# A windowed attention and gated MLP kernel: loads in 1 KB runs, half-width chunks in pairs, another mask operation, layer-norm apply on GpSimd

## The chip, the cores and the metric

The kernel runs on one core of a Trainium2 chip. The time is the device time in microseconds of one execution; lower is better. The core has TensorE (PE), VectorE (DVE), ScalarE (ACT), GpSimd (POOL) and SyncE (SP), each with an instruction queue of its own that runs in the order of the program.

## The reference, cut to what matters

The inputs are float32; B=8 batches, H=8 heads, S=576 tokens, D=64. Attention looks back over 64 tokens only, and its output, heads side by side, goes through a spatial gating unit.

```python
scores = (q @ k^T) / sqrt(64)                # per batch and head, 576 x 576
mask   = (rel >= 0) & (rel < 64)             # rel = query position - key position
attn   = softmax(where(mask, scores, -1e9))
x      = attn @ v                            # heads side by side: (8, 576, 512)

h      = relu(x @ w_in)                      # (8, 576, 1024)
u, v   = h[..., :512], h[..., 512:]
v_n    = (v - mean(v)) / sqrt(var(v) + 1e-6) # over the 512 features
v_s    = w_spatial @ v_n + b_spatial         # mixes the 576 tokens
out    = (u * v_s) @ w_out                   # (8, 576, 512) float32
```

## The kernel before, in words

All of a batch's work is cut into units, and a list written out by hand gives each engine its order; nothing is scheduled at run time. The 576 tokens are four chunks of 128 and a remainder of 64; heads go in pairs, so that a batch has attention steps s=0 to 3 (two heads each, 512 tokens) and s=4 (the last 64 tokens of all heads).

Per batch b the units are:

- Loads: q, k and v come from DRAM in float32 on SP's queue (some of batch 0's v on ACT's). In DRAM a head's rows of 64 floats follow each other; a load puts token 128c+p on partition p, so each DMA moves runs of 256 bytes. Batches 0 and 1 are loaded head by head (`load_heads`, L68), later ones by chunk (`load_chunk`, L76). There are two buffers for each of q, k and v, in float32 (`NAT`) and in float16 (`F16`, names hq, hk, hv).
- Casts to float16 (`cast_pair` L81, `cast_chunk` L88), and a second copy hs of v that is moved by 64 tokens (`shift_pair` L93 and L94, `shift_half` L103 and L104), on POOL; batch 0 has its k casts on ACT and its q casts on DVE.
- T(b,s): PE transposes of k and q into the PSUM tile tp, which DVE copies to qk (L216).
- S(b,s): 16 small matmuls make the scores of key blocks of 64 tokens against at most 128 queries, in tile sc. E(b,s): ACT takes the exponential (L264), and DVE applies the mask by a `min` against a tile that holds 0 where a key isn't seen and 65504 where it is (L270).
- P(b,s): two matmuls with a matrix of ones (onesK, L281) sum the exponentials, and 16 matmuls of 64 columns (L290) multiply with v, both into oz. N1 and N2: ACT takes the logarithm of the sums and the exponential of minus that (L298, L306), and DVE multiplies (L308), which gives x.
- V(b,j), j=0 to 4: the half of the first product that is normalised, one chunk of tokens at a time; ACT's ReLU (L333) and DVE's `bn_stats` and `bn_aggr` (L335, L336). V(b,4) has only 64 tokens.
- LN(b): ACT takes Ln and Exp for the inverse deviations (L343, L344), then DVE applies the normalisation to the five chunks by a `tensor_scalar` each (L352, tiles vn).
- U(b,m): the other half (L362, L368) and its ReLU (L364). G(b,m): the product with the transposed w_spatial (wspT) and a row that adds the bias (L382, L390), then DVE multiplies with U's result. Each G reads all five vn.
- O(b,j): the last product (L403), a copy by ACT (L406) and the store (L407), which stands in ACT's queue for batches 0 and 1 and in SP's after that. O(b,4) has 64 tokens.

PSUM holds one tile each of tp, sc and oz, and three of tag mm, which V, U, G and O share. At the start PE also runs matmuls on a scratch tile (`warm`, L114).

Batch 0's attention comes first, then its V, W (the transposes of w_spatial), LN and U; then batch 1's attention with batch 0's G and O between the steps. In the main loop, iteration i has batch i's attention steps 0 to 4, and between them O of batch i-2 in step 0, V of batch a=i-1 in step 1, LN, U and the first G of batch i-1 in step 2, and the other U and G in steps 3 and 4. Loads and casts of batch i+1 are issued in the same iteration.

Of the kernel before, what the change touches and what calls it, by code (L numbers as in the profile page):

```python
# [13 lines left out]
B = 8  # L14
S = 576
BIG = 65504.0


@with_exitstack
def kernel(  # L20
# [31 lines left out]

    NAT = {}
    F16 = {}

# [8 lines left out]
    SRC = (q, k, v)  # L64

    def load_heads(b, x, h0, eng):
        for h in (h0, h0 + 1):
            eng.dma_start(NAT[b][x][:, 0:4, h, :],  # L68
                          SRC[x][b, h, 0:512, :].rearrange("(c p) d -> p c d", p=128))
# [4 lines left out]
    def load_chunk(b, x, c):  # L74
        sn = 128 if c < 4 else 64
        nc.sync.dma_start(NAT[b][x][0:sn, c, :, :],  # L76
                          SRC[x][b, :, 128 * c:128 * c + sn, :].transpose([1, 0, 2]))

    def cast_pair(b, x, p, eng):
        hs = slice(2 * p, 2 * p + 2)  # L80
        eng.tensor_copy(F16[b][x][:, 0:4, hs, :], NAT[b][x][:, 0:4, hs, :])  # L81

    def cast_rem(b, x, eng):
        eng.tensor_copy(F16[b][x][0:64, 4, :, :], NAT[b][x][0:64, 4, :, :])

    def cast_chunk(b, x, c, eng):
        sn = 128 if c < 4 else 64
        eng.tensor_copy(F16[b][x][0:sn, c, :, :], NAT[b][x][0:sn, c, :, :])  # L88
# [7 lines left out]
    def shift_rem(b, eng):  # L96
        eng.tensor_copy(F16[b][3][0:64, 4, :, :], F16[b][2][0:64, 4, :, :])

    def shift_half(b, half, eng):
        vn, vs = F16[b][2], F16[b][3]  # L100
        c = 2 * half
        if half < 2:
            eng.tensor_copy(vs[0:64, c:c + 2, :, :], vn[0:64, c:c + 2, :, :])  # L103
            eng.tensor_copy(vs[64:128, c + 1:c + 3, :, :], vn[64:128, c:c + 2, :, :])  # L104
        else:
            eng.tensor_copy(vs[0:64, 4, :, :], vn[0:64, 4, :, :])
# [9 lines left out]
    def load_by_pairs(b):  # L116
        new_batch(b)
        for p in range(4):
            for x in (1, 0, 2):
                load_heads(b, x, 2 * p, nc.scalar if (b == 0 and p < 2 and x == 2) else nc.sync)  # L120
        for x in (1, 0, 2):
            load_rem(b, x, nc.sync)

    load_by_pairs(0)
    new_half(0)
    warm(16)
# [16 lines left out]
    mask = cpool.tile([128, 2, 8, 64], f16, name="mask")  # L143
    maskr = cpool.tile([128, 8, 64], f16, name="maskr")
    for h in (0, 1):
        for u in range(8):
            if u % 2 == 1:
                nc.vector.tensor_copy(mask[:, h, u, :], keep[:])
            else:
                nc.vector.tensor_scalar(mask[:, h, u, :], keep[:], -1.0, BIG, ALU.mult, ALU.add)  # L150
        nc.vector.memset(mask[64:128, h, 0, :], 0.0)
    for u in range(8):
        nc.vector.tensor_copy(maskr[:, u, :], mask[:, 0, 2, :])
# [4 lines left out]
    for i in range(NSB):  # L158
        nc.vector.memset(mv_t[i][:], 1.0)
        nc.vector.memset(vn4_t[i][64:65, :], 1.0)  # L160

    def casts_step(b, s, engk, engq):
        if s < 4:
            cast_pair(b, 1, s, engk)
            cast_pair(b, 0, s, engq)
            cast_pair(b, 2, s, nc.gpsimd)
            shift_pair(b, s, nc.gpsimd)
        else:
            for x in (1, 0, 2):
                cast_rem(b, x, nc.gpsimd)  # L170
            shift_rem(b, nc.gpsimd)

    class _Act:
        @staticmethod
        def tensor_copy(o, i):
            nc.scalar.copy(o, i)  # L176
# [4 lines left out]
    wsp_nat = [cpool.tile([128, 576], f16, name=f"wnat{t}") for t in range(5)]  # L181
# [6 lines left out]
    def load_wsp():  # L188
        for t in range(5):
            tn = 128 if t < 4 else 64  # L190
            nc.gpsimd.dma_start(wsp_nat[t][0:tn, :], moe_w_spatial[128 * t:128 * t + tn, :])
        nc.gpsimd.dma_start(wspT[4][64:65, 0:576], moe_b_spatial[:].unsqueeze(0))
# [9 lines left out]
    X = {}  # L202

    def emit_T(b, s):
        tp = psp.tile([128, 1024], f16, tag="tp", bufs=1, name=f"tp{b}_{s}")
        Qh, Kh = F16[b][0], F16[b][1]
        with nc.named_scope(f"T{b}_{s}"):
            if s < 4:
# [7 lines left out]
                nc.vector.tensor_copy(qk[:, :], tp[:, :])  # L216
# [11 lines left out]
    SC = {}  # L228

    def emit_S(b, s):  # L230
# [3 lines left out]
        with nc.named_scope(f"S{b}_{s}"):  # L234
            if s < 4:
                for kap in range(8):
                    r = 64 * (kap % 2)
                    c0 = 0 if kap == 1 else 64 * kap
                    c1 = min(512, 64 * kap + 128)
                    for h in (0, 1):  # L240
                        d = slice(64 * h, 64 * h + 64)
                        nc.tensor.matmul(sc[r:r + 64, h, c0:c1],  # L242
                                         qk[d, 512 + 64 * kap:576 + 64 * kap], qk[d, c0:c1],
                                         start=True, stop=True)
            else:
                for p in range(4):
                    for h in (0, 1):
                        d = slice(64 * h, 64 * h + 64)
                        qs = qk[d, 64 * p:64 * p + 64]
                        nc.tensor.matmul(sc[0:64, h, 64 * p:64 * p + 64],  # L250
                                         qk[d, 256 + 64 * p:320 + 64 * p], qs,
                                         start=True, stop=True)
                    for h in (0, 1):
                        d = slice(64 * h, 64 * h + 64)
                        qs = qk[d, 64 * p:64 * p + 64]
                        nc.tensor.matmul(sc[64:128, h, 64 * p:64 * p + 64],
                                         QK[b, p][d, 960:1024], qs,
                                         start=True, stop=True)

    def emit_E(b, s):  # L260
        sc = SC.pop((b, s))
        if s < 4:
            e2 = apool.tile([128, 2, 512], f16, tag="e2", bufs=2, name=f"e2_{b}_{s}")
            nc.scalar.activation(e2[:, :, :], sc[:, :, :], AF.Exp, bias=0.0, scale=0.125)  # L264
            m = mask[:, :, :, :].rearrange("p h u w -> p h (u w)")
# [52 lines left out]
    G = {}  # L318
# [245 lines left out]
```

The softmax here doesn't subtract the row's maximum and nothing guards it: scores larger than these inputs give would overflow.

## Time and profile before

| | |
|---|---|
| three runs | 250.28, 251.56, 252.69 us; median 251.56 us |
| the profiled execution | 251.05 us, of which its instructions span 249.3 us |
| mean granted clock of PE | 0.962 of full speed |
| busy: PE, DVE, ACT, POOL | 227.3, 155.3, 152.2, 122.1 us |
| moved by DMA | 40.41 MB in 120014 packets, 113776 of them under 512 bytes |

Busy shares are means over stages that have different limits. A busy PE is one whose queue had a matmul in flight; the granted clock tells how fast it went. "x" ahead of a number is a count of instructions, an arrow with a name in square brackets tells what ended an idle time.

### The profile page before, as it was taken

To read this page: it belongs to the slowest core of one execution; us is meant where nothing else is said; L and a number is where in the kernel's file an instruction comes from. 1 tells how busy PE (TensorE), PEld (TensorE's weight loads), DVE (VectorE), ACT (ScalarE), POOL (GpSimd) and SP (SyncE) were. 2 spreads that over 40 slices of the span, in tenths; PEclk is the share of its full clock that TensorE was granted. 3 is DMA by queue.
4 is the path that set the end of the run, shared out by engine and by line. 5 is a ranking of instruction groups with operands and counts; after the bars stand their busy time and mean duration, and the time that the engine had idled before them with its cause. 6 is when DMAs were issued, how large, how long until landed. Compare 5 with 4: busy or idle time off the path is not lost.

```text
span 249.3 us, 6391 instructions
## 1 busy us (share of the span) xinstructions
PE 227.3 (91%) x2588; PEld 116.8 (47%) x2588; DVE 155.3 (62%) x317; ACT 152.2 (61%) x266; POOL 122.1 (49%) x183
## 2 busy tenths in 40 slices
PE   7784996996399999999999999999999999999893
PEld 3442453553254464436544554455445544553351
DVE  6453277562459782887479556966597659755630
ACT  3373484446447666766785577756776677767423
POOL 3469638875499695369016592469135900000000
PEclk9999799799569999999999999999999999999998
DMA  8999999999999996992389948995499040014005
GB/s 159 218 184 208 216 204 229 191 201 276 249 199 210 198 178 175 246 206 52 128 192 211 192 128 221 189 198 135 137 216 156 27 165 5 3 42 149 0 3 189
DMA packets 120014, 40.41 MB, mean 162 GB/s; under 512 B 113776, under 2 KB 114864, under 8 KB 119984
## 3 DMA queue, kind: packets, MB, share of 16 engines
q1 hardware_dynamic: 114720, 34.88, 70.1%
q0 software_dynamic: 1840, 2.24, 5.2%
q10 hardware_dynamic: 3424, 2.88, 4.1%
q8 instruction: 20, 0.33, 0.6%
q14 instruction: 10, 0.08, 0.1%
HBM read 32.79 MB, written 9.44 MB: 169 GB/s over the span
## 4 chain that ended last, share of the span: by engine, by line
PE 60%; DVE 13%; ACT 9%; DMA 8%; SPq 3%; POOL 2%; issue 2%; ACTq 1%; POOLq 0%
SPq L68 3%; DMA nv_80<-in_v_dram 2%; DMA out_dram<-ob_0_1033 2%; DMA out_dram<-ob_1_3433 2%; DMA nq_78<-in_q_dram 2%; ACTq L407 1%; PE ps_0_804 L382 1%; PE warm_583 L114 1%; PE pv_0_1308 L330 1%; PE ps_0_4590 L382 1%; PE ps_0_4237 L382 1%; DVE mv_172 L336 1%; PE ps_0_3720 L382 1%; PE ps_1_895 L382 0%; PE ps_3_4653 L382 0%
## 5 line engine op out<-in xcount | busy, mean ns | idle before, releaser
L88 POOL CAST hq_2281<-nq_2285 128x512 f16<-128x512 f32 (+1 forms) x5 | 3.2, 635 | 12.8 <-DMA nq_2285<-in_q_dram 12.8
L114 PEld LDWEIGHTS <-scratch 128*128 128x128 f16 x51 | 5.0, 112 | 7.3 <-issue 3.8
L88 POOL CAST hq_3389<-nq_3393 128x512 f16<-128x512 f32 (+1 forms) x5 | 3.9, 797 | 8.8 <-DMA nq_3393<-in_q_dram 8.8
L281 PEld LDWEIGHTS <-onesK 128*64 128x64 f16 x80 | 4.6, 107 | 7.5 <-issue 5.2
L88 POOL CAST hq_2835<-nq_2839 128x512 f16<-128x512 f32 (+1 forms) x5 | 3.6, 720 | 8.3 <-DMA nq_2839<-in_q_dram 8.3
L176 ACT CAST hk_109<-nk_79 128x512 f16<-128x512 f32 x4 | 2.5, 618 | 7.5 <-DMA nk_79<-in_k_dram 7.5
L114 PE MATMUL warm_113<-scratch 128*128 128x512 f16 x16 | 5.5, 524 | 1.3 <-DVE scratch L109 1.3
L81 POOL CAST hv_110<-nv_80 128x512 f16<-128x512 f32 x4 | 2.5, 632 | 8.3 <-DMA nv_80<-in_v_dram 7.3
L88 POOL CAST hv_1729<-nv_1733 128x512 f16<-128x512 f32 (+1 forms) x5 | 3.5, 708 | 4.4 <-DMA nv_1733<-in_v_dram 4.4
L88 POOL CAST hq_1727<-nq_1731 128x512 f16<-128x512 f32 (+1 forms) x5 | 2.9, 609 | 4.6 <-DMA nq_1731<-in_q_dram 4.6
L88 POOL CAST hv_2283<-nv_2287 128x512 f16<-128x512 f32 (+1 forms) x5 | 3.2, 637 | 3.8 <-DMA nv_2287<-in_v_dram 3.8
L81 POOL CAST hv_433<-nv_437 128x512 f16<-128x512 f32 x4 | 2.5, 613 | 5.2 <-DMA nv_437<-in_v_dram 5.1
L88 POOL CAST hv_1184<-nv_764 128x512 f16<-128x512 f32 (+1 forms) x5 | 3.1, 611 | 3.9 <-DMA nv_764<-in_v_dram 3.9
L362 PEld LDWEIGHTS <-win_181 128*128 128x128 f16 x32 | 3.1, 98 | 3.8
L362 PEld LDWEIGHTS <-win_182 128*128 128x128 f16 x32 | 3.1, 98 | 3.8
L88 POOL CAST hv_1220<-nv_1224 128x512 f16<-128x512 f32 (+1 forms) x5 | 3.9, 780 | 2.0 <-DMA nv_1224<-in_v_dram 2.0
L88 POOL CAST hq_1182<-nq_762 128x512 f16<-128x512 f32 (+1 forms) x5 | 3.3, 654 | 3.2 <-DMA nq_762<-in_q_dram 2.7
L81 DVE CAST hq_108<-nq_78 128x512 f16<-128x512 f32 x4 | 1.7, 432 | 4.8 <-DMA nq_78<-in_q_dram 4.8
L281 PE MATMUL oz_3_1153<-e_1_3_1108,onesK 128*64 128x512 f16 x2 | 0.6, 611 | 4.4 <-DVE x_2_1133 L308 4.4
L88 POOL CAST hv_3391<-nv_3395 128x512 f16<-128x512 f32 (+1 forms) x5 | 3.0, 611 | 2.8 <-DMA nv_3395<-in_v_dram 2.8
L88 POOL CAST hv_2837<-nv_2841 128x512 f16<-128x512 f32 (+1 forms) x5 | 3.3, 666 | 2.0 <-DMA nv_2841<-in_v_dram 1.8
L264 ACT ACTIVATE e_1_0_831<-sc_0_813 128x1024 f16<-128x1024 f32 x1 | 1.0, 1023 | 5.2 <-PE sc_0_813 L242 5.2
(1871 smaller groups left out, 940.3 us busy)
## 6 DMA issues: line engine op xcount, KB each, us to landing
nk_79<-in_k_dram SPq DMA_DIRECT2D x9, 128.0 KB, 3.9
nq_78<-in_q_dram SPq DMA_DIRECT2D x9, 128.0 KB, 4.1
nk_436<-in_k_dram SPq DMA_DIRECT2D x9, 128.0 KB, 4.8
nq_435<-in_q_dram SPq DMA_DIRECT2D x9, 128.0 KB, 4.8
nv_437<-in_v_dram SPq DMA_DIRECT2D x9, 128.0 KB, 4.1
nk_763<-in_k_dram SPq DMA_DIRECT2D x4, 256.0 KB, 5.5
nq_762<-in_q_dram SPq DMA_DIRECT2D x4, 256.0 KB, 5.7
nv_764<-in_v_dram SPq DMA_DIRECT2D x4, 256.0 KB, 6.0
```

Of the source, the lines that this page charges most:

```text
L68: eng.dma_start(NAT[b][x][:, 0:4, h, :], SRC[x][b, h, 0:512, :].rearrange("(c p) d -> p c d", p=128))
L81: eng.tensor_copy(F16[b][x][:, 0:4, hs, :], NAT[b][x][:, 0:4, hs, :])
L88: eng.tensor_copy(F16[b][x][0:sn, c, :, :], NAT[b][x][0:sn, c, :, :])
L114: nc.tensor.matmul(t[:, :], scratch[:, 0:128], scratch[:, :], start=True, stop=True)
L176: nc.scalar.copy(o, i)
L264: nc.scalar.activation(e2[:, :, :], sc[:, :, :], AF.Exp, bias=0.0, scale=0.125)
L281: nc.tensor.matmul(oz[64 * h:64 * h + 64, 1, 0:n], onesK[:, :], e2[:, h, 0:n], start=True, stop=True)
L330: nc.tensor.matmul(pv[0:jn, :], xcol(b, r, j), w_in_sb[r][:, 512:1024], start=(r == 0), stop=(r == 3))
L336: nc.vector.bn_aggr(mv_t[b % NSB][0:jn, j, :], st6[0:jn, 0:6])
L362: nc.tensor.matmul(pu[:, :], w_in_sb[r][:, 128 * m:128 * m + 128], X[b, r][:, :], start=(r == 0), stop=(r == 3))
L382: nc.tensor.matmul(ps[:, :], VN[b, kk][0:kn, 128 * m:128 * m + 128], wspT[kk][0:kn, 0:512], start=(kk == 0), stop=(kk == 4))
L407: (nc.scalar if b < 2 else nc.sync).dma_start(out[b, 128 * j:128 * j + jn, :], ob[0:jn, :])
```

## The change

It changes the layout of the loads, the order of the units, and the engine or operation of three steps:

- q of all batches, and k of batches 0 to 2 (`KRUNS = 3`), are loaded so that partition p holds tokens 4p to 4p+3 of a head, one run of 1 KB. Casts of such tensors go head by head. So tokens of q stand in another order (4p+j in column 128j+p); scores, masks, x, w_spatial and the output rows follow that order: S and P's matmuls with v read and write four runs instead of one, DVE copies k's transposes in two parts for those batches, the transposes of w_spatial read every fourth column, and the store writes rows 4p+j. w_spatial's first 512 rows come in one DMA, and the bias goes through a tile brow and two ACT copies.
- Loads go out one iteration earlier (batch i+2's in iteration i); casts go by head pairs in all batches, batch 2's during batch 1's attention.
- V(a,4) and O(o,4) become one unit VO4 with the two products on the two halves of one PSUM tile. O's other chunks and V are spread over steps 0 to 2, and all G are in steps 3 and 4.
- The mask is applied by `scalar_tensor_tensor` (max with 0, then min with the mask).
- LN is applied as v*rs+nb, with nb = -mean*rs from a small DVE instruction, and on POOL for all batches but 0.

```diff
+    def in_runs(b, x):
+        return x == 0 or (x == 1 and b < KRUNS)
+
+    def load_runs(b, x, h0, n, eng):
+        eng.dma_start(NAT[b][x][:, 0:4, :, :].rearrange("p j h d -> p (j h d)")
+                      .rearrange("p (h e) -> p h e", h=8)[:, h0:h0 + n, :],
+                      SRC[x][b, h0:h0 + n, 0:512, :].rearrange("h (p j) d -> p h (j d)", j=4))
...
     def cast_pair(b, x, p, eng):
-        hs = slice(2 * p, 2 * p + 2)
-        eng.tensor_copy(F16[b][x][:, 0:4, hs, :], NAT[b][x][:, 0:4, hs, :])
+        if in_runs(b, x):
+            src = NAT[b][x][:, 0:4, :, :].rearrange("p j h d -> p (j h d)") \
+                .rearrange("p (h j d) -> p j h d", h=8, j=4)
+            for h in (2 * p, 2 * p + 1):
+                copy_on(eng, F16[b][x][:, 0:4, h, :], src[:, :, h, :])
+        else:
+            hs = slice(2 * p, 2 * p + 2)
+            copy_on(eng, F16[b][x][:, 0:4, hs, :], NAT[b][x][:, 0:4, hs, :])
...
-                nc.vector.tensor_copy(qk[:, :], tp[:, :])
+                if in_runs(b, 1):
+                    nc.vector.tensor_copy(qk[:, 512:1024].rearrange("d (p j) -> d p j", j=4),
+                                          tp[:, 512:1024].rearrange("d (j p) -> d p j", j=4))
+                    nc.vector.tensor_copy(qk[:, 0:512], tp[:, 0:512])
+                else:
+                    nc.vector.tensor_copy(qk[:, :], tp[:, :])
...
-        nc.vector.tensor_tensor(e2[:, :, :], e2[:, :, :], m, ALU.min)
+        nc.vector.scalar_tensor_tensor(e2[:, :, :], e2[:, :, :], 0.0, m, ALU.max, ALU.min)
...
+    def emit_VO4(a, o):
+        pv = mm(f"pvo{a}_{o}")
+            for r in range(4):
+                if a is not None:
+                    nc.tensor.matmul(pv[0:64, :], X[a, 4][:, 64 * r:64 * r + 64],
+                                     w_in_sb[r][:, 512:1024], start=(r == 0), stop=(r == 3))
+                if o is not None:
+                    nc.tensor.matmul(pv[64:128, :], G[o, 4][:, 64 * r:64 * r + 64],
+                                     w_out_sb[r][:, :], start=(r == 0), stop=(r == 3))
+        if a is not None:
+            v_tail(a, 4, pv)             # ReLU, bn_stats, bn_aggr
+        if o is not None:
+            nc.scalar.copy(ob[64:128, :], pv[64:128, :])
+            store_eng(o).dma_start(out[o, 512:576, :], ob[64:128, :])
...
-            nc.vector.tensor_scalar(vn[0:jn, :], vs[0:jn, :], mv[0:jn, j, 0:1],
-                                    rs[0:jn, j:j + 1], ALU.subtract, ALU.mult)
+            (nc.vector if b < 1 else nc.gpsimd).tensor_scalar(
+                vn[0:jn, :], vs[0:jn, :], rs[0:jn, j:j + 1], nb[0:jn, j:j + 1], ALU.mult, ALU.add)
...
     # main loop, iteration i with a = i - 1, o = i - 2 (o > 0, a < B)
+            st[0] += Os(o, (0, 1)) + Vs_(a, (0, 1))
+            st[1] += Vs_(a, (2, 3)) + [lambda: emit_VO4(a, o)] + Os(o, (2,))
+            st[2] += [lambda: emit_LN(a)] + Os(o, (3,)) + Us(a, (0, 1, 2))
+            st[3] += Gs(a, (0,)) + Us(a, (3,)) + Gs(a, (1,)) + Us(a, (4,))
+            st[4] += Gs(a, (2, 3, 4))
+        loads = load_units(i + 2)        # four of them ahead of each step
+        casts = cast_units(i + 1)        # step s: head pair s; in step 2 they stand ahead of LN
```

The line numbers L81 to L407 above are those of the kernel before. In the changed kernel the mask is L300, the layer-norm apply L400, the small instruction for nb L392, the copies of qk L245, L247 and L249, the casts L119 and the shifts L137 and L138.

## The prediction, made before the changed kernel was run

> **What bounds the kernel now.** I read the page's busy shares and slices first, then the busy time by stretches, then PE's timeline in one steady iteration, then POOL's timeline and the DMA queues.
>
> ```profile
> span 249.3 us, 6391 instructions
> PE 227.3 (91%) x2588; PEld 116.8 (47%) x2588; DVE 155.3 (62%) x317; ACT 152.2 (61%) x266; POOL 122.1 (49%) x183
> ...
> PEclk9999799799569999999999999999999999999998
> DMA  8999999999999996992389948995499040014005
> ```
> ```profile
> 42.00:68.00 26.00, 20.11 (x272) 11.56 (x272) 11.98 (x20) 12.72 (x20) 16.83 (x27) 0.84 1.20 229
> 68.00:92.70 24.70, 24.02 (x303) 13.35 (x303) 18.65 (x35) 15.25 (x27) 21.33 (x27) 0.89 1.10 203
> ...
> 118.90:145.00 26.10, 25.65 (x315) 13.27 (x314) 18.42 (x36) 18.16 (x33) 9.44 (x14) 1.00 0.96 183
> ```
> The first columns are the stretch and its length, then busy time of PE, PEld, DVE, ACT, POOL, PE's granted clock, DMA share, GB/s. From 92.7 us on PE is busy 98% at full clock: iterations i=3 to 6 of the main loop take 26.0 us each (92.7 to 196.7), i=7 24.6, the tail 28.0. Before that the DMA engines are never idle, at about 200 GB/s, and PE waits and loses clock. So there are two stages with different limits: a stream of loads up to 92.7, and PE after it.
>
> ```profile
> 126.69 0.41 PE L281 MATMUL oz_0_2456<-e_4_0_2358,onesK 128*64 128x512 f16 x2
> 126.93 0.23 PE L290 MATMUL oz_0_2456<-e_4_0_2358,hv_1729 128*64 128x64 f16 x4
> ...
> 129.11 0.40 PE L330 MATMUL pv_4_2507<-win_179,x_4_2383 128*64 128x512 f16 x1
> 129.35 0.38 PE L330 MATMUL pv_4_2507<-win_180,x_4_2383 128*64 128x512 f16 x1
> ...
> 133.34 0.39 PE L382 MATMUL ps_0_2612<-wspT_192,vn_0_2544 128*128 128x512 f16 x1
> 133.67 0.39 PE L382 MATMUL ps_0_2612<-wspT_193,vn_1_2546 128*128 128x512 f16 x1
> 134.28 0.39 PE L382 MATMUL ps_0_2612<-wspT_194,vn_2_2548 128*128 128x512 f16 x1 [0.23 <-DVE vn_2_2548 L352]
> 134.60 0.39 PE L382 MATMUL ps_0_2612<-wspT_195,vn_3_2550 128*128 128x512 f16 x1
> 135.22 0.39 PE L382 MATMUL ps_0_2612<-wspT_196,vn_1_174 65*128 65x512 f16 x1 [0.23 <-DVE vn_1_174 L352]
> ```
> Full-width matmuls of 512 columns start 0.216 us apart. The two onesK matmuls, each 64 columns of the array and writing opposite halves of PSUM, together hold PE only from 126.69 to 126.93: 0.24 us for two. So half-width pairs run side by side, while V4 and O4 alone (one half each) still pay 0.216 a matmul. And G0 takes 2.2 us from 133.34 to 135.54 instead of 1.08: it waits for the five vn from DVE.
>
> **The change by parts.**
>
> *Pairing (VO4).* O4 or V4 costs four matmuls and a pause of 0.09 at the switch of width, 0.95 us. As a pair one of them vanishes, seven times (o=0 to 6); in i=3 to 7 and in the tail this is on PE's path: -0.95 each. Its ReLU, bn_stats, output copy and store remain, the store on ACT's queue for o<2 and else SP's.
>
> *Later need for vn.* G moves from step 2 to step 3, so that after VO4 PE has O2, T, O3, S and P, U0 to U2 and T4 first: 0.87+0.45+0.87+1.0+2.6+0.35, about 6.3 us with switches, before G0 starts.
>
> *Layer-norm apply on POOL (L400).* Five DVE tensor_scalars (start spacing 0.33, or 0.70 beside POOL) go away for batches 1 to 7, one small DVE nb is added (0.15, by the aggregate's 0.18). POOL's price for it is not in the trace. Nearest rows: a 128x512 POOL cast 0.61; affine_select 0.24 for 64 and 0.29 for 128 columns, a slope of 0.8 ns a column, 0.60 for 512. Lower end 0.61; upper end a second pass over the data, 0.18+2x0.43=1.03 (0.61 and the 1.03 of a 64x1024 copy give fixed 0.18 and 0.43 per 512). I take 0.65: it streams one tensor like the cast.
>
> The Trainium skill speaks against this (GPSIMD Engine Reference, § 3.1): software loops there reach 1.8 cycles an element at best above two operations, 0.77 us for 512 elements; by that estimate each of seven LNs would be 0.6 us later and the sum 4 us worse. The casts' 0.61 is faster than that loop, so the row decides.
>
> *Is vn in time?* With t0 at a step-0 T, PE reaches VO4's end at 8.9. ACT then has relu, the output copy, ln, O2's copy and zi before Ln and Exp: rs at 12.1. DVE has x and the qk copy ahead of nb: 13.0. POOL from 13.1 at 0.65: vn4 at 16.4, wanted by G0's fifth matmul at 16.1. But POOL's queue holds the casts of steps 0 to 2 in front. Per pair: k 0.61, q two casts of 256 elements (0.40 each by that slope), v 0.61, two shifts 1.22: 3.24 us; the shift of pair 0 waits for P(i-1,4) at about 3.0. 3.0+1.2+2x3.24=10.7, inside 13.0 if little is lost to DVE. So G0 stalls 0.2 at best, 1.1 more for each mask that holds POOL up. I take 0.7 against 1.1 now. Behind LN on POOL stand casts of steps 3 and 4 (5.7 us); T(i+1,3), four steps or some 19 us later, needs them, and that covers them; loads now go out a whole iteration ahead on SP's queue, so the stores queued between them cost nothing.
>
> *Mask op (L300).* The f16 tensor_tensor shows 0.69 (starts 0.60 apart). No row shows a scalar_tensor_tensor; ends 0.60 and 1.13 (the 0.60 that 512 f32 elements take, less fixed 0.07, doubled, plus 0.07), I take 1.13: +0.53 on DVE, four times an iteration, against 5x0.33 to 0.70 saved; DVE stays near 18 of 25 us. Exp's end to P's use leaves 3 us now, so +0.5 is hidden; without that cover it costs 0.5 a step.
>
> ```profile
> 87.19 1.32 DVE L270 TENSOR_TENSOR e_2_3_1589<-e_2_3_1589,mask 128x1024 f16<-128x1024 f16 x1 [0.73 <-ACT e_2_3_1589 L264]
> ...
> 88.03 1.39 POOL L104 COPY hs_1221<-hv_1220 64x1024 f16<-64x1024 f16 x1
> ```
> Here a mask beside a POOL copy takes 1.32 instead of 0.69, and the next copy 1.39 instead of 1.03: they exclude each other. The Trainium skill (SBUF — State Buffer, § Who interferes with whom) says that any DVE op with two SBUF inputs contends with a POOL op that reads SBUF; the new op still has two, so by the rule a mask would now hold POOL 1.1 us and the stall would be 1.3, by which the sum would be some 3 us worse.
>
> *Four-run streams.* S and PV matmuls read and write four runs of 16 or 32 instead of one. No row shows it; ends are today's 0.35+0.27 a step and twice that. I take today's: the column count is unchanged.
>
> *k's two copies (L245, L247)* for batches 0 to 2: 0.60+0.33 against 0.60 on DVE, idle half of that stage. Bias copies on ACT (about 0.8) ahead of LN(0), masks behind the first q cast (about 1 us), fewer and larger weight DMAs: all in the fill, hidden by the stream below; uncovered, 2 us.
>
> *1 KB runs.*
> ```profile
> q1 hardware_dynamic: 18774, 4.72, 107.5%
> q10 hardware_dynamic: 656, 1.18, 13.4%
> ```
> This is the DMA view of 44 to 70 us: 256-byte packets (q1) take 24 ns each, 2 KB stores (q10, 576 of them) 97 ns. On a line between them a 1 KB packet takes 55, so 1.74 times the bytes a second: 348 GB/s against 200. q or k of a batch (1.05 MB) then needs 3.0 us instead of 5.2. Ends: 200 (no gain) and 490 (q1's 4.72 MB at 200 fill 23.6 of the 26 us, which leaves 2.4 for the stores' 1.18 MB).
>
> **The fill, which now ends on POOL.** Batch 3's last v lands at 86 now:
> ```profile
> 86.38 0.61 POOL L88 CAST hv_1220<-nv_1224 64x512 f16<-64x512 f32 x1 [0.18 <-DMA nv_1224<-in_v_dram]
> ```
> Seven tensors (q of batches 0 to 3, k of 0 to 2) gain 2.2 us: 70.4, its last chunk 69.4. v is still loaded by chunks and cast by pairs, so pair 0's v cast waits for all of it, and LN(1) stands in POOL's queue behind pairs 0 to 2 of batch 3: 69.4+0.61+1.22+2x3.24=77.7, five vn 81.0, G0(1) done 81.3. PE would have been there at about 70 (T(2,1) at 58: POOL's last cast for batch 2 waits for v landing at about 52). After G0 come 8 us of PE work plus 1.9 for a clock lost in the 11 us pause (42.65 to 46.2 now shows such a stretch at 0.43 spacing): i=3 starts at 91.2, now 92.7: -1.5. So most of the faster load is handed back as POOL's wait. Ends: without gain in rate 107 (+14); at 490 POOL's own work allows LN(1) at 70, i=3 at 83 (-10).
>
> **Sum.** Fill -1.5; i=3 to 6: -(0.95+0.4)x4=-5.4; i=7 -1.0; tail -0.95 for the pair and nothing net for LN (DVE's 0.33 becomes 0.65, more PE work lies before G0). Total -8.8: span 249.3 to 240.5, the profiled run 251.05 (1.75 outside the span) to 242.2, and against the median of 251.56, 242.8.
>
> **Rivals.**
> *LN on POOL becomes the bound (slower).* Place: vn before G0. Each 0.1 us on L400 costs 0.5 in seven places (LN(1), i=3 to 7, tail), 3.5 us; it takes the gain away from 0.90 us an op; at 1.03 it is 13.3-8.8=+4.5, 256.1. For: POOL's queue is nearly full (15.4 casts, 3.3 LN, some 4 lost to masks, of 25). Against: one-input rows stream at 0.8 ns. 14%.
> *POOL keeps up in the fill*: i=3 at 83, 8 us more gained: 234.6. For: stores seem nearly free beside loads. Against: three batches of casts in line. 22%.
> *1 KB runs no faster* (the change doesn't do what it says): i=3 at 107, +15.6: 258.4. For: HBM or issue could be the limit; against: SP issues 256 KB in 1.05 us unblocked but needs 1.2 here, so the engines are slow. 8%.
> *Four-run streams at twice the time*: 0.62x4x5=+12.4: 255.2. 6%.
>
> **Numbers.** Forecast 50%, its own range 237 to 249. The range 231 to 257 adds the quick fill and most of the POOL case. A measurement here tells about 1%, so faster is under 249.0: forecast and quick fill and a small part of the POOL case, 0.76; within 1% 0.08; slower 0.16.
>
> **What would show it.** Right: L400 near 0.65; POOL idle before a v cast of batch 3 ended by DMA; G0(1) waiting several us for POOL; po_0_ of iteration 3 near 91; later iterations near 24.7 with G0 close to 1.8; both halves of VO4 in 0.9 us. Wrong: L400 above 0.9, S groups longer than 0.35, or batch 3 landing far from 70.

## The result and the profile after

The changed kernel is slower. Its four runs took 259.86 to 262.98 us, median 261.61, against 250.92 for the kernel before beside it: a ratio of 1.041, 95% interval 1.032 to 1.051. The prediction was 242.8, range 231 to 257. Here and below the times are medians of all runs, while ratios and their intervals leave out the executions in a second, slower state, some per cent longer. The profiled execution took 260.86 us, of which its instructions span 259.1.

The first and second parts of the page of the changed kernel:

```profile
span 259.1 us, 6474 instructions
PE 220.0 (85%) x2586; PEld 117.0 (45%) x2586; DVE 165.8 (64%) x298; ACT 152.3 (59%) x272; POOL 172.8 (67%) x275
...
DMA  7999999999999809990587858680220023002304
```

PE is busy for 7.3 us less than before (at 0.95 each, seven pairs make 6.7 of it), and the span is 9.8 us longer: PE waits more. The DMA engines' first empty slice is the fifteenth, 91 to 97 us, so that from there on loads don't hold the rest up. POOL went from 122 to 173 us of work. Two stretches of the same kernel show it by stage (columns: length, busy PE, PEld, DVE, ACT, POOL, PE's granted clock, DMA share, GB/s):

```profile
73.00:99.45 26.45, 23.44 (x300) 12.15 (x299) 19.21 (x33) 16.18 (x29) 24.01 (x38) 0.90 0.78 168
...
129.30:155.40 26.10, 24.19 (x315) 13.21 (x314) 18.82 (x32) 17.84 (x32) 22.06 (x33) 1.00 0.74 183
```

In the first stretch, which is i=2, POOL is busy for 24 of 26 us. The second is one steady iteration, from S(4,0) to S(5,0). It takes 26.1 us like before, with 24.2 of PE work instead of 25.7. So the pair's gain is there and is waited away.

The table gives the start of some S groups and the span, all from PE's timelines, for this kernel, the one before and the experiments; "steady" is a third of S(4,0) to S(7,0).

| | S(0,1) | S(1,0) | S(2,0) | S(3,0) | S(4,0) | S(7,0) | span | steady |
|---|---|---|---|---|---|---|---|---|
| before | 11.8 | 44.8 | 69.3 | 94.4 | 120.5 | 198.3 | 249.3 | 25.9 |
| changed | 14.8 | 49.7 | 75.9 | 101.3 | 129.3 | 207.7 | 259.1 | 26.1 |
| e1 | 14.8 | 47.0 | 70.0 | 95.0 | 123.5 | 200.2 | 249.0 | 25.6 |
| e2 | 13.7 | 44.8 | 71.2 | 99.5 | 127.3 | 203.5 | 254.1 | 25.4 |
| e3 | 12.9 | 44.1 | 75.5 | 100.9 | 129.3 | 207.7 | 259.1 | 26.1 |
| e4 | 14.3 | 46.9 | 70.6 | 94.7 | 122.5 | 197.0 | 245.5 | 24.8 |
| e5 | 14.1 | 45.3 | 70.5 | 100.8 | 129.1 | 210.1 | 261.0 | 27.0 |
| e6 | 14.3 | 47.0 | 71.9 | 93.8 | 118.2 | 189.4 | 236.9 | 23.7 |
| e7 | 13.6 | 45.2 | 72.0 | 94.1 | 117.8 | 189.0 | 236.9 | 23.7 |
| e10 | 14.8 | 47.5 | 70.5 | 94.6 | 120.2 | 196.8 | 245.3 | 25.5 |
| e11 | 14.3 | 46.6 | 69.6 | 92.1 | 115.8 | 187.0 | 234.5 | 23.7 |
| e12 | 11.2 | 43.7 | 70.3 | 92.4 | 116.1 | 187.3 | 234.8 | 23.7 |
| e13 | 11.6 | 44.2 | 65.6 | 86.9 | 110.9 | 182.1 | 229.2 | 23.7 |
| e14 | 11.9 | 43.3 | 67.6 | 89.1 | 113.6 | 184.8 | 231.8 | 23.7 |

Of the 9.8 us that the changed kernel is late at the end, 6.9 are there at S(3,0) and 1.9 more at S(4,0). Less than 1 us is added after that.

Each row is one execution, and its start varies. Up to S(2,0) the changed kernel, e1 and e5 have the same instructions in the same order. Yet S(1,0) comes at 49.7, 47.0 and 45.3 us in them and S(2,0) at 75.9, 70.0 and 70.5. Part of it is ACT's fourth copy of batch 0's output, which waits for the first store to land in the changed kernel and waits for nothing in e1:

```profile
68.14 0.59 ACT L455 COPY ob_3_1152<-po_3_1146 128x512 f32<-128x512 f32 x1 [3.34 <-DMA out_dram<-ob_0_1059]
```
```profile
62.65 0.58 ACT L455 COPY ob<-po 128x512 f32<-128x512 f32 x1
```

So a difference of a few us between two rows at S(1,0) or S(2,0) shows nothing by itself. The steady column and the medians over the runs are firmer. The places where time is lost are three.

**A steady iteration on PE** (i=4; the timeline's columns are start, duration, engine, line, operation; the bracket is the idle time ahead and what ended it):

```profile
134.97 0.38 PE L373 MATMUL pvo_2_2510<-win_139,x_4_2423 128*64 128x512 f16 x1
135.00 0.38 PE L376 MATMUL pvo_2_2510<-wout_143,g_4_2310 128*64 128x512 f16 x1
...
135.97 0.39 PE L452 MATMUL po_2_2530<-wout_143,g_0_2127 128*128 128x512 f16 x1
...
139.73 0.41 PE L311 MATMUL oz_1_2607<-e_4_1_2507,onesK 128*64 128x512 f16 x2 [1.07 <-DVE x_0_2541 L339]
...
143.35 0.39 PE L430 MATMUL ps_0_2680<-wspT_150,vn_0_2571 128*128 128x512 f16 x1
...
144.57 0.39 PE L430 MATMUL ps_0_2680<-wspT_153,vn_3_2577 128*128 128x512 f16 x1 [0.36 <-POOL vn_3_2577 L400]
145.31 0.39 PE L430 MATMUL ps_0_2680<-wspT_154,vn_1_138 65*128 65x512 f16 x1 [0.36 <-POOL vn_1_138 L400]
```

The halves of VO4 start 0.03 us apart, and O2 starts at 135.97: two units in 1.0 us. But P(4,1) then waits 1.07 us for x_0, because there is one oz tile and x_0 is the last reader of the P before. And G0 takes 2.2 us, from 143.35 to the start of the next unit at 145.54, where five matmuls need 1.08: 1.1 us of waiting for vn, just as before the change. So 0.95 is gained and 1.07 is lost, with 0.2 more for x_4 ahead of P(4,0).

**LN of the same iteration on POOL:**

```profile
140.52 0.77 POOL L400 TENSOR_SCALAR vn_0_2571<-vs_0_2403,rs_2566,nb_2567 128x512 f16<-128x512 f16 x1 [0.71 <-DVE nb_2567 L392]
141.27 1.73 POOL L400 TENSOR_SCALAR vn_1_2573<-vs_1_2416,rs_2566,nb_2567 128x512 f16<-128x512 f16 x1
...
144.50 0.76 POOL L400 TENSOR_SCALAR vn_1_138<-vs_4_2520,rs_2566,nb_2567 64x512 f16<-64x512 f16 x1
```
```profile
140.83 1.54 DVE L300 SCALAR_TENSOR_TENSOR e_4_2_2627<-e_4_2_2627,mask 128x1024 f16<-128x1024 f16 x1 [0.48 <-ACT e_4_2_2627 L294]
```

One apply takes 0.77 us, and in every LN but the last one of them is held up to 1.6 to 1.8 us, by the mask that DVE starts meanwhile (the second fence): the apply that starts at 141.27 ends 0.63 us after the mask does. All five take 4.7 us instead of the 3.3 of the prediction.

**Why x_0 is late** is seen on ACT, in the same iteration:

```profile
136.13 0.59 ACT L354 ACTIVATE vs_4_2520<-pvo_2_2510 64x512 f16<-64x512 f32 x1 [0.48 <-PE pvo_2_2510 L376]
136.75 0.58 ACT L382 COPY ob_4_2525<-pvo_2_2510 64x512 f32<-64x512 f32 x1
137.35 0.60 ACT L329 ACTIVATE ln_0_2528<-oz_0_2487 128x512 f32<-128x512 f32 x1
137.85 0.58 ACT L455 COPY ob_2_2536<-po_2_2530 128x512 f32<-128x512 f32 x1
138.31 0.64 ACT L337 ACTIVATE zi_0_2539<-ln_0_2528 128x512 f32<-128x512 f32 x1
```

P(4,0) is done at 135.0, but N1 (ln_0) stands in ACT's queue behind VO4's ReLU and output copy, and N2 (zi_0) behind O2's copy. In iterations 2 and 3 the stores are issued on ACT too, and the same wait is 2.1 to 2.2 us.

**The start** (POOL's timeline from the landing of batch 2's v to the first LN on POOL):

```profile
56.52 0.62 POOL L119 CAST hv_784<-nv_608 128x512 f16<-128x512 f32 x1 [7.65 <-DMA nv_608<-in_v_dram]
...
73.32 0.61 POOL L119 CAST hk_1232<-nk_794 128x512 f16<-128x512 f32 x1
...
75.05 0.62 POOL L119 CAST hv_1233<-nv_795 128x512 f16<-128x512 f32 x1 [0.43 <-PE pv_0_1260 L364]
...
78.12 1.48 POOL L119 CAST hk_1232<-nk_794 128x512 f16<-128x512 f32 x1
...
82.25 1.48 POOL L119 CAST hk_1232<-nk_794 128x512 f16<-128x512 f32 x1
...
86.52 1.58 POOL L400 TENSOR_SCALAR vn_0_1460<-vs_0_1266,rs_1455,nb_1456 128x512 f16<-128x512 f16 x1 [0.21 <-DVE nb_1456 L392]
```

From 56.5 POOL has only 1.8 us of idle time until LN(1). (The profile puts the 0.43 us ahead of the cast at 75.05 down to PE. But the last chunk of batch 3's v, which this cast needs, was issued at 69.5, and at the 5.3 us that such a load takes it landed at about 74.8, so that this wait may have been for the load.) Three pairs of batch 3 take 13.0 us, 73.3 to 86.3, or 4.3 a pair: the first has two waits of 1.5 us together, and in the second and third a cast of 0.61 has become one of 1.48 beside a mask (77.53 to 79.13 and 81.92 to 83.25 on DVE).

### The profile page after: what moved, and what is told of

Read it like the earlier page. It is cut to its first block, busy times and chain, and to the rows that moved or that the text cites. A ratio compares the mean times of both kernels' runs of the same rounds, so it can differ in the third digit from the quotient of the medians.

```text
span 259.1 us, 6474 instructions
## 1 busy us (share of the span) xinstructions
PE 220.0 (85%) x2586; PEld 117.0 (45%) x2586; DVE 165.8 (64%) x298; ACT 152.3 (59%) x272; POOL 172.8 (67%) x275
## 4 chain that ended last, share of the span: by engine, by line
PE 52%; POOL 12%; DVE 12%; ACT 12%; DMA 5%; issue 5%; ACTq 1%; POOLq 0%; SPq 0%
DMA out_dram<-ob_0_1059 3%; DMA nq_78<-in_q_dram 2%; POOL vn_1_138 L400 1%; DMA out_dram<-ob_1_4740 1%; POOL vn_0_137 L400 1%; PE ps_0_810 L430 1%; DVE maskr L194 1%; PE warm_304 L158 1%; POOL vn_1_2013 L400 1%; PE pv_0_1260 L364 1%; POOL vn_1_4201 L400 1%; POOL vn_1_3679 L400 1%; POOL vn_1_3133 L400 1%; POOL vn_1_2573 L400 1%; POOL vn_0_1460 L400 1%
## 5 line engine op out<-in xcount | busy, mean ns | idle before, releaser
L311 PEld LDWEIGHTS <-onesK 128*64 128x64 f16 x80 | 6.0, 107 | 19.5 <-issue 16.9
L400 POOL TENSOR_SCALAR vn_0_4595<-vs_0_4520,rs_4590,nb_4591 128x512 f16<-128x512 f16 x1 | 0.8, 773 | 17.3 <-PE pu_0_4613 L410 17.3
L400 POOL TENSOR_SCALAR vn_0_4199<-vs_0_4051,rs_4194,nb_4195 128x512 f16<-128x512 f16 x1 | 0.8, 772 | 14.7 <-DVE nb_4195 L392 14.7
L119 POOL CAST hv_102<-nv_80 128x512 f16<-128x512 f32 (+1 forms) x5 | 5.0, 997 | 5.4 <-DMA nv_80<-in_v_dram 5.3
L119 POOL CAST hv_784<-nv_608 128x512 f16<-128x512 f32 (+1 forms) x5 | 3.1, 613 | 7.7 <-DMA nv_608<-in_v_dram 7.7
L119 POOL CAST hq_782<-nq_606 128x256 f16<-128x256 f32 (+1 forms) x9 | 4.6, 533 | 2.3 <-DMA nq_606<-in_q_dram 2.3
L119 POOL CAST hk_1232<-nk_794 128x512 f16<-128x512 f32 (+1 forms) x5 | 5.7, 1131 | 0.2
L137 POOL COPY hs_1761<-hv_1760 64x512 f16<-64x512 f16 x4 | 3.3, 828 | 3.0 <-PE oz_4_1822 L324 2.8
L117 ACT CAST hk_101<-nk_79 128x256 f16<-128x256 f32 x8 | 2.8, 400 | 3.9 <-DMA nk_79<-in_k_dram 3.9
L410 PEld LDWEIGHTS <-win_141 128*128 128x128 f16 x32 | 3.2, 101 | 4.1 <-issue 0.6
L410 PEld LDWEIGHTS <-win_142 128*128 128x128 f16 x32 | 3.2, 101 | 4.1 <-issue 0.6
L119 POOL CAST hk_2319<-nk_1763 128x512 f16<-128x512 f32 (+1 forms) x5 | 4.8, 961 | 0.2
L119 POOL CAST hk_3439<-nk_2883 128x512 f16<-128x512 f32 (+1 forms) x5 | 4.8, 961 | 0.2
L119 POOL CAST hk_2879<-nk_2323 128x512 f16<-128x512 f32 (+1 forms) x5 | 4.8, 961 | 0.2
L119 POOL CAST hk_417<-nk_421 128x256 f16<-128x256 f32 (+1 forms) x9 | 4.5, 527 | 0.3
L119 DVE CAST hq_100<-nq_78 128x256 f16<-128x256 f32 x8 | 2.1, 300 | 4.0 <-DMA nq_78<-in_q_dram 4.0
L119 POOL CAST hq_1758<-nq_1235 128x256 f16<-128x256 f32 (+1 forms) x9 | 4.6, 531 | 0.0
L410 PEld LDWEIGHTS <-win_140 128*128 128x128 f16 x32 | 3.3, 102 | 2.9 <-issue 0.3
```

Source lines behind the costliest of these rows:

```text
L119: eng.tensor_copy(o, i)
L137: eng.tensor_copy(vs[0:64, 0:4, hs, :], vn[0:64, 0:4, hs, :])
L311: nc.tensor.matmul(oz[64 * h:64 * h + 64, 1, 0:n], onesK[:, :], e2[:, h, 0:n], start=True, stop=True)
L400: (nc.vector if b < 1 else nc.gpsimd).tensor_scalar(vn[0:jn, :], vs[0:jn, :], rs[0:jn, j:j + 1], nb[0:jn, j:j + 1], ALU.mult, ALU.add)
L410: nc.tensor.matmul(pu[:, :], w_in_sb[r][:, 128 * m:128 * m + 128], X[b, r][:, :], start=(r == 0), stop=(r == 3))
```

## The experiments

Fifteen more kernels were run. In e1 to e3 and e5 the edit is to the changed kernel alone; the others say what they are built on.

### e1: LN on DVE

```diff
-            (nc.vector if b < 1 else nc.gpsimd).tensor_scalar(
+            nc.vector.tensor_scalar(
```

> The changed kernel with the layer-norm apply of all batches on DVE, all else as changed. Theory A (two waits share the loss of the steady iterations: G0 waits about 1.1 us for vn because LN on POOL needs 4.7 us, and P(i,1) waits about 1.1 us for x_0, which stands behind VO4's ReLU and copy on ACT): only the first goes, 1.1 us in i=3 to 7, 0.7 in i=2 and about 2 in the tail, some 8 us, so 253 to 255, with the wait for x_0 still there or longer. Theory B (LN on POOL is the whole loss): 251 or less. Theory C (POOL's price doesn't matter, DVE with the long masks is what is late): 260 to 264.

Measured: 253.35 us, ratio to before 1.006 (1.002 to 1.010). That is 8.3 us less than the changed kernel, as theory A had it; theory B's full loss is not reached. The steady iteration only falls to 25.6, by half of theory A's 1.1 us: G0's wait is gone and x_0's is not. In the profiled executions 6.3 us of the gain stand at S(3,0), but 5.9 of them are there at S(2,0) already, where the instructions are still the same. So the number came out as theory A had it, but not from the places that it named.

### e2: the old mask

```diff
-        nc.vector.scalar_tensor_tensor(e2[:, :, :], e2[:, :, :], 0.0, m, ALU.max, ALU.min)
+        nc.vector.tensor_tensor(e2[:, :, :], e2[:, :, :], m, ALU.min)
```

> The changed kernel with the mask applied by the old tensor_tensor min, all else as changed. Theory A: the mask falls from 1.23 to 0.69 us and holds POOL up by about 0.6 instead of 1.1 us, so that vn comes 0.5 us earlier and x_4 and x_0 some 0.3 to 0.5 earlier; 0.7 us in each of six iterations and the tail, 256 to 258. Theory C (DVE with the long masks is what is late): 251 to 254. If the masks are hidden altogether: 260 to 263.

Measured: 256.11 us, 1.014 (1.004 to 1.024): 5.5 us less. The mask was not hidden.

### e3: the masks early

```diff
-    run(c0[0])
     build_masks()
+    build_maskr()                # and the four memsets of mv_t and vn4_t
+    run(c0[0])
```

> The changed kernel with the masks, maskr and the four memsets built on DVE ahead of the first q cast, where DVE waits for the first load from 1.3 to 5.3 us. Theory A (the first batches are one chain through PE, ACT and DVE, and the 5 us that G0 of batch 0 is late are carried to the end): S(0,1) moves from 14.8 to about 11.8 and the time falls by 2 to 4 us, to 258 to 260. Theory D (POOL's queue, busy without a break from the landing of batch 2's v at 56.5 to the vn of batch 1 at 91, ends this stage): no change, 261 to 262.

Measured: 261.64 us, 1.037 (1.028 to 1.047): no change. S(0,1) comes 1.9 us and S(1,0) 5.6 us earlier, and at S(2,0) all but 0.4 of it is gone. Not all of the 5.6 is the edit's: over the rows of the table S(1,0) lies at 44.8 to 49.7 with the masks late and at 43.3 to 44.2 with the masks early. Something after S(1,0) stops PE until a time of its own. That speaks for theory D as far as the outcome goes. That it is POOL alone this run doesn't show: ACT too stood still in it, four times 0.7 to 3.5 us around the issues of batch 0's stores.

### e4: both, LN on DVE and the old mask

The two edits of e1 and e2 together.

> The changed kernel with both the layer-norm apply on DVE and the old tensor_tensor mask; what stays is the layout, the loads, VO4 and the order. If the two are separate costs: the sum of the two gains, 249 to 252. If both only cure the same wait of G0 for vn: as with LN on DVE alone, 253 to 255, because the wait for x_0 and the late start remain. Theory B: under 249.

Measured: 247.43 us, 0.983 (0.975 to 0.991). From e1 to e4 the mask is worth 5.9 us, from e2 to e4 the place of LN 8.7; the two costs add up. The steady iteration:

```profile
122.50:147.30 24.80, 23.78 (x315) 13.14 (x314) 19.08 (x36) 17.82 (x32) 16.18 (x28) 1.00 0.83 193
```

So layout, loads, pairs and order without these two make the kernel 1.7% faster than before (0.9 to 2.5% by the interval), and PE still waits 1.0 us an iteration.

### e5: N1 and N2 ahead of VO4

```diff
-                att_step(i, s, st[s], 2, 1, nxt)
+                att_step(i, s, st[s], 2, 0 if s == 1 else 1, nxt)
```

> The changed kernel with N1 and N2 of step 0 put ahead of VO4 and O2 in step 1 (ACT's and DVE's order alone; PE's stays), LN still on POOL and the mask as changed. Theory A, the two waits are in series: x_0 comes about 1 us earlier, but the fifth bn_stats, and with it nb and all vn, come some 0.6 us later, so that G0 waits longer by what P(i,1) waits less: 260 to 263. Rival: the wait for x_0 costs its 1.1 us in i=4 to 7 and 2.1 in i=2 and 3 whatever LN does: 253 to 255.

Measured: 262.98 us, 1.049 (1.042 to 1.056). As theory A had it, nothing is won while vn is late. PE's waits for vn in this run, over the whole span and from 97 to 235 us (total, count, longest):

```profile
PE ps L430 <- POOL vn L400: 12.3, 19, 4.2
```
```profile
PE ps L430 <- POOL vn L400: 7.1, 15, 0.8
```

In the changed kernel x_0 cost PE five waits of 1.1 to 2.2 us in the same stretch. Here x has 1.0 us left in two, and G0's waits have grown from 3.5 to 7.1. The longest wait for vn, 4.2 us, lies ahead of this stretch, in i=2.

### e6: the same on top of e4

> The kernel of the experiment with LN on DVE and the old mask (247.4), with N1 and N2 of step 0 ahead of VO4 and O2 in step 1. Theory A: with vn no longer late, the wait for x_0 is what is left: 1.1 us less in i=4 to 7 and about 2 less in i=2 and 3, 240 to 243. Rival: DVE's later bn_stats and the five vn on DVE take it back: 246 to 249.

Measured: 239.26 us, 0.952 (0.948 to 0.956): 8.2 us less than e4, more than expected. The same edit that changed nothing for the better with LN on POOL (1.4 us more) now gains 8.2. The steady iteration:

```profile
118.20:142.00 23.80, 23.80 (x319) 13.04 (x318) 19.21 (x37) 17.74 (x32) 16.10 (x28) 1.00 0.83 200
```

PE is busy without a break in it. Iteration 3 falls from 27.8 to 24.4 us.

### e7: batch 1's stores on SP

```diff
-        return nc.scalar if b < 2 else nc.sync
+        return nc.scalar if b < 1 else nc.sync
```

> As the one before, and the stores of batch 1 on SP's queue instead of ACT's. Theory A: each issue of a store holds ACT for about 0.8 us (0.4 of issue, 0.4 until the copy's end), five of them in i=3: 1 to 2 us less than without this edit, 239 to 242. Rival: behind the loads in SP's queue the stores land late, ob's three buffers are full and ACT waits for them: 2 us or more slower than without.

Measured: 238.27 us, 0.947 (0.943 to 0.951), 1.0 less than e6. It is the low end of what was expected, and the two intervals overlap.

### e8: the new mask alone, in the kernel before

```diff
-        nc.vector.tensor_tensor(e2[:, :, :], e2[:, :, :], m, ALU.min)
+        nc.vector.scalar_tensor_tensor(e2[:, :, :], e2[:, :, :], 0.0, m, ALU.max, ALU.min)
```

> The kernel before with one edit: the mask by scalar_tensor_tensor. If the longer mask is hidden, as the prediction said (3 us between the exponential and its use): 251 to 252. If it costs there what it cost in the changed kernel (5.7 us, as it holds up DVE and, through the shared access, POOL): 255 to 258.

Measured: 253.23 us, 1.007 (1.003 to 1.010). There it costs 2 us: nearly hidden, as the prediction said, in the order in which the prediction had looked at it.

### e9 and e15: LN on POOL, in the kernel before

e9 moves the `tensor_scalar` of L352 to POOL for batches 1 to 7 as it stands, `(v - mean) * rs`. e15 moves it in the form of the change, `v * rs + nb`, with nb from DVE.

> The kernel before with one edit: the layer-norm apply of batches 1 to 7 on POOL. There G0 follows LN at once, so that each 0.4 us that one apply takes longer (0.75 instead of 0.35) stands on PE's path, and so do the 1 us of a mask in between and whatever casts stand ahead in POOL's queue. Theory A: 5 x 0.4 or some 2 to 3 us for each of seven batches, 265 to 272. If LN on POOL is hidden there: 251 to 253.

> The kernel before with LN on POOL as in e9_before_ln_pool (358.9), but in the form of the change, v*rs+nb with nb from DVE, instead of subtract and multiply. If the 2.07 us of one apply there came from the form: 0.77 us an op and 6.5 us less for each of seven batches, 300 to 315. If it came from the place (the neighbours on POOL and DVE in that order): 2 us an op and 350 to 360 again.

Measured: e9 358.86 us, 1.432 (1.423 to 1.441), far outside what was expected; e15 311.73, 1.241 (1.233 to 1.248), as expected. The group of L352 in e9 and that of the same operation in e15 (count, busy time, mean ns of one, idle time before and its releasers):

```profile
L352 POOL TENSOR_SCALAR vn<-vs,mv,rs 128x512 f16<-128x512 f16 x28 | 57.7, 2068 | 57.1 <-DVE qk L216 33.7 <-ACT rs L344 23.4
```
```profile
L354 POOL TENSOR_SCALAR vn<-vs,rs,nb 128x512 f16<-128x512 f16 x28 | 22.0, 798 | 56.2 <-DVE nb L346 56.2
```

So the form was the cause of the 2.07: all 35 applies of e9 take 2.06 to 2.08 us as subtract and multiply, while multiply and add takes 0.77 (0.80 with those held up). The two forms differ in the operations and in the scalars that they read, and which of these it is was not tried. The 61 us that remain in e15 are put down to the place, without a run of its own: POOL's casts of the next batch's q stand ahead of LN and in i=5 wait 14.1 us for a load of the same iteration, and PE waits 37.9 us in all for vn. In the changed kernel, with its loads an iteration earlier, the profile names no load that POOL waits for after 56.5 us.

### e10: the new mask on the fast kernel

e7 with the `scalar_tensor_tensor` again.

> The fastest kernel so far (LN on DVE, old mask, N1 and N2 first, stores of batch 1 on SP; 238.3) with the scalar_tensor_tensor mask again. If the mask costs by being one step of the chain to x_0, which is no longer late: hidden but for the fill, 238 to 241. If it costs as in the changed kernel by DVE's time: 243 to 245.

Measured: four runs from 247.06 to 252.77 us, and no ratio; the two lowest, 247.06 and 247.18, are 8.9 us above e7's 238.27. This is more than both expectations. A mask takes 0.5 us longer (means of 1.33 in e1 and 0.81 in e4), four times an iteration. A steady iteration of e7 and one of e10:

```profile
117.80:141.60 23.80, 23.80 (x319) 13.06 (x322) 19.03 (x36) 17.74 (x32) 16.10 (x28) 1.00 0.84 201
```
```profile
120.20:145.80 25.60, 24.32 (x319) 13.45 (x318) 21.42 (x37) 17.83 (x32) 17.70 (x28) 1.00 0.79 187
```

DVE has 2.4 us more work, the iteration is 1.8 longer. DVE isn't full, but it runs its queue in order, and what stands behind a mask (x, the bn_stats, g) comes later, to PE's waits. PE waited for g in L430 in this kernel, which e7's waits don't show. POOL's work also grew by 1.6 us without a single instruction more. Beside e1, which has the new mask and LN on DVE too, e10 with N1 and N2 first gains nothing in the steady iteration (25.5 to 25.6 in both): in three iterations the waits for x fall from 3.8 to 0.7 us, and 2.0 us of waits for g come. So the cure of e6 needs the old mask as well.

### e11, e12, e13: the fill

e11 is e7 with all stores on SP (`return nc.sync`). e12 adds e3's edit. e13 adds a fourth output buffer, for which lnz gives up one of its two:

```diff
-        ob = mpool.tile([128, 512], f32, tag="ob", bufs=3, ...)
+        ob = mpool.tile([128, 512], f32, tag="ob", bufs=4, ...)
-        lnz = apool.tile([128, 512], f32, tag="lnz", bufs=2, ...)
+        lnz = apool.tile([128, 512], f32, tag="lnz", bufs=1, ...)
```

> The fastest kernel so far with batch 0's stores too on SP's queue. Theory D (what is left in the fill is ACT, which stands still when its store is not taken or has not landed beside the load stream, between S(1,3) at 57.5 and S(2,0) at 72): S(2,0) comes 4 to 6 us earlier, 233 to 236. Rival: SP now waits for O's copies and the loads behind its stores come later, or ob's buffers are freed later still: 238 to 242.

> As the one before, with the masks and memsets ahead of the first q cast. Where the stores no longer tie ACT to the load stream, the 3 to 5 us by which S(1,0) comes earlier should reach the end: 230 to 234. If the stage is bound by the loads or by POOL's casts of batch 2 (57 to 73 us in the changed kernel): no more than 1 us from the one before.

> As the one before (stores on SP, masks early; 236.4), with four buffers ob instead of three (the room comes from a second buffer of lnz that its one engine doesn't need). Theory D in its narrower form (in the fill ACT's fourth output copy waits 4.4 us for the first store to land, and P(1,3) waits behind it 5.8 us for x_2): that wait goes, S(2,0) moves from 70.3 to about 65, and the time to 231 to 234. Rival (POOL's casts of batch 2 or the loads end the fill next): no more than 1 us, 235 to 237.

Measured: e11 235.85 us, 0.942 (0.937 to 0.947); e12 236.41, 0.942 (0.938 to 0.946); e13 231.69, 0.925 (0.922 to 0.928). In e11 S(2,0) moved by 2.4 us, less than expected and no more than the starts of one kernel differ by; the time fell by as much. In e12 the earlier masks bring S(1,0) 2.9 us forward and nothing at S(2,0). ACT's timeline in e12, and the same copy in e13:

```profile
57.13 1.03 ACT L294 ACTIVATE e<-sc 128x1024 f16<-128x1024 f32 x1
62.53 0.58 ACT L455 COPY ob<-po 128x512 f32<-128x512 f32 x1 [4.37 <-DMA out_dram<-ob]
```
```profile
59.06 0.59 ACT L455 COPY ob<-po 128x512 f32<-128x512 f32 x1 [0.39 <-PE po L452]
```

The fourth copy waited for the first store to land beside the load stream, and N1, N2, x_2 and P(1,3) waited behind it (5.8 us on PE in e12, 1.9 in e13). With a fourth buffer S(2,0) is at 65.6 and the time 4.7 us lower: theory D in the narrower form. e13 is the fastest kernel here.

### e14: k in 256-byte runs

e13 with `KRUNS = 0`.

> As e13_four_ob, with k of batches 0 to 2 in 256-byte runs again (KRUNS = 0), casts and copies of k as for the other batches. If the load stream's rate sets the fill: three k of 1.05 MB at 200 instead of 337 GB/s, 2.1 us each, up to 6 us later. If ACT, PE and POOL set it: within 2 us, or faster, as DVE has one copy of qk less to make and POOL one cast instead of two.

Measured: 233.65 us, 0.933 (0.930 to 0.937), 2.0 us more than e13. So with those walls gone the 1 KB runs of three tensors are worth 2.0 us in all, the shorter copies and casts of the 256-byte form set against them, of the 6.3 us by which they should load faster at the two measured rates. What q's runs are worth by themselves was not tried.

## Why the prediction was wrong

**Right.** The pair: two units take 1.0 us. The way to vn in the steady iteration: from step 0's T (127.00 in i=4) POOL was to start the applies at 13.1 and starts at 13.5, and the stretch from VO4 to G0 is the 6.3 us of the forecast and x_0's wait. The four-run streams cost nothing: S(4,0) to the P behind it takes 0.34 us, and S(4,0) was 0.35 before. The rate of 1 KB runs, taken from a line between two packet sizes as 348 GB/s (all of the time of q10 was put on 576 of its 656 packets, which moves the line by little): the DMA view of the changed kernel over 2 us of q alone but for some of v, and over 4 us of 256-byte packets, gives

```profile
DMA packets 780, 0.67 MB, mean 337 GB/s; under 512 B 155, under 2 KB 780, under 8 KB 780
...
DMA packets 3139, 0.80 MB, mean 199 GB/s; under 512 B 3138, under 2 KB 3138, under 8 KB 3138
```

And the mask's price, 1.13 taken, 1.23 measured where nothing holds it up.

**Wrong: the price of LN on POOL (0.65 taken, 0.77 measured, 1.7 for one of five).** The prediction reasoned from the 0.61 us of a cast and set aside the Trainium skill (GPSIMD Engine Reference, § 3.1), whose estimate was 0.77 for 512 elements. The measurement is 0.77, which agrees with the page's figure; the nearest row was a row of another operation. The figure isn't for every form: subtract and multiply took 2.07 (e9). The hold-up by a mask was priced from a row and from the skill (SBUF — State Buffer, § Who interferes with whom: two SBUF inputs on DVE exclude a POOL instruction that reads SBUF), and then only the milder value was chosen. It came in six of the seven LNs: 1.58 to 1.81 us. So the five vn took 4.7 us instead of 3.3. The sum had -0.4 an iteration for G0's stall; it stayed at 1.1. The first rival (LN on POOL becomes the bound, 14%) named this place, with 3.5 us for each 0.1 us on an apply. By its own rule 0.12 us more is 4.2 us, and with the hold-up (4.7 for five, 0.95 an apply) it is 10.5; e1 gives 8.3.

**Wrong: the mask at nothing.** Its price was right, and the cover named for it (3 us between the exponential and P) was mostly real in the old order: e8 costs 2 us. The step left out was that every later instruction in DVE's queue is moved too (waits for g in e10), and that POOL is shut out for longer (its 1.6 us in e10). From e1 to e4 the cost is 5.9 us; how it divides between the two is not shown.

**Wrong: nobody waits behind VO4.** The working listed what ACT has to do after VO4 and before Ln and Exp of LN, to find when vn comes. It didn't ask the same of N1 and N2, which stand in the same list, and of the one oz tile that P needs. This is the wait that took the place of the one removed: 1.07 us in i=4 to 7 and 2.1 to 2.2 in i=2 and 3, and no rival named it. Alone it can't be cured (e5), because then vn is the later one. With LN on DVE and the old mask its cure gives 8.2 us (e6 beside e4), with LN on DVE and the new mask nothing in the steady iteration (e10 beside e1). So the waits stood in line, and one cure was hidden by the next wait.

**Wrong: the fill (-1.5 taken, +6.7 measured at O0 of i=3: 99.45).** The mechanism was named rightly, LN(1) in POOL's queue behind the casts of batch 3's pairs 0 to 2, and its terms were too small. By the prediction the last chunk of batch 3's v lands at 69.4, and pair 0's cast and shifts and two pairs of 3.24 us bring LN(1) to 77.7. It started at 86.5, 8.8 us later. Of these, 5.6 are there at pair 0's v cast (75.05): POOL was busy with batch 2's casts up to 73.3 and then with pair 0's k and q, since batch 2's v had landed at 56.5 instead of about 52; and batch 3's last chunk of v landed at about 74.8. Why the loads came so much later than at the rate that was rightly forecast, no run tells. 1.1 more is the wait of pair 0's shift for P(1,4), and 1.7 are the casts of the next two pairs that were held up by a mask; without a hold-up a pair does take 3.24 (91.07 to 94.31). Then the five applies took 4.6 instead of 3.3, and O0 followed G0(1) by 8.1 us, as reckoned without the lost clock. The 11 us pause on PE did not come, since PE itself was late by then: in this execution G0(1) starts at 89.3 and loses 1.0 us to vn.

There are two walls here, then. With LN on POOL S(3,0) lies at 99.5 to 101.3 (e2, e3, e5 and the changed kernel), whether S(2,0) is at 70.5 or at 75.9, and with LN on DVE at 93.8 to 95.0 (e1, e4, e6). e1 and e5 reach S(2,0) within 0.5 us of each other, and then take 25 and 30 us to S(3,0), with the 4.2 us wait for vn in e5 (which has N1 and N2 first as well). That POOL is a wall for S(3,0) is shown by this. In the changed kernel's own profiled execution the start was late enough to give 101.3 without it (75.9 and the 25 us of an iteration). That second wall, the edits in the first 25 us and the stores on ACT's queue, the sum had priced at nothing. With the masks behind the first cast S(1,0) comes about 3 us later (the middle of the rows is 46.9 with them late and 43.9 with them early); behind it the wait for the stores hides that (e12). Only with the fourth buffer, and LN on DVE, does S(2,0) come at 65.6 (e13); what the early masks are worth there was not tried apart.

**The tail** was to be 0.95 shorter: from S(7,3) at 224.7 to the end it is 34.4 us, before 34.2. The pair is there, and G0(7) waits three times for vn on POOL, 0.3 to 0.4 us each. With LN on DVE the same stretch is 32.9 (e1) and 32.6 (e4).

**In sum:** the 242.8 of the forecast needed a steady iteration of 24.65. It is 24.8 once LN and mask are as before (e4), and this is partly chance: the wait for x_0, 1.0 us, which the sum lacks, stands where it had kept 0.7 for G0's. The two edits to LN and mask cost 14.2 us, and they were put at -1.6 and 0. By place, the span that was forecast, 240.5, is missed by 18.6 us: some 8.2 at the start of i=3, some 8 from there to S(7,0), and some 2.4 after it.

## What to carry to other kernels

When a unit is put into a queue, list everything that stands behind it in every engine's queue, not only the chain that the unit itself feeds: here the norm of the attention, behind an output copy on ACT, cost as much as the whole gain. Move work to POOL only with a price measured for that operation in that form, beside the DVE instructions that will run with it. And when one of several suspected waits is taken away without effect, take two away together before calling it harmless: e5 lost 1.4 us and e6, the same edit on e4, gained 8.2. And profile one kernel's start more than once before reading a few us in it: three executions of the same instructions reached S(2,0) at 70.0, 70.5 and 75.9 us.

## What the runs showed of the hardware that was not expected

- A `tensor_scalar` of 128x512 float16 on POOL with two per-partition scalars takes 0.77 us as multiply and add (changed kernel, e15) and 2.07 us as subtract and multiply (e9).
- 1 KB runs load at 337 GB/s (2 us in which 155 of 780 packets are of 256 bytes) and 256-byte runs at 199, measured in one kernel.
- A 128x1024 float16 mask by `scalar_tensor_tensor` takes 1.23 us on DVE, by `tensor_tensor` 0.69. Beside it a POOL apply of 0.77 us lasts up to 1.81 and a cast of 0.61 up to 1.48 or 1.6, and the wait counts as busy time of POOL (16.1 us in e7, 17.7 in e10, 28 instructions each).
- A store that is issued beside the load stream takes 7.2 us to land (ob_0 of batch 0 in the changed kernel) against 2.3 to 2.9 for batches 5 to 7, and ACT stood still for up to 3.5 us around the issue of such a store (e3).
